# Strassen's seven products for gate and value of layer two

## The chip, the cores and the metric

The kernel runs on one core of one Trainium2 chip. The metric is the device time of one execution in microseconds (us), and lower is better. Each number stands for a median over executions. TensorE (PE) does the matmuls, VectorE (DVE) the elementwise work on two operands, ScalarE (ACT) activations and copies, GpSimd (POOL) one subtraction, and SyncE (SP) issues the DMAs.

## The reference, cut to what matters

An attention with a window and block sums feeds two layers, one after the other. The change touches the second layer, and the end of the first.

```python
def _moe_ref(x, w_in, w_out):                  # layer one: x 1536x512, d_ff 2048
    h = x @ w_in
    g = h * (1.0 / (1.0 + np.exp(-1.702 * h)))
    return (g @ w_out).astype(np.float32)

def _moe2_ref(x, w_gate, w_val, w_out):        # layer two: d_ff 1536
    gate = 1.0 / (1.0 + np.exp(-(x @ w_gate)))
    val = x @ w_val
    return (gate * val @ w_out).astype(np.float32)
```

The weights are double precision in memory.

## The kernel before

**Operands.** Every operand of a matmul is held as two tiles, a rounded high part and the low rest (`xH`, `xL`, `gh`, `gl`, and hi and lo of each weight). `mm3` (line 176) computes a product as three matmuls into one PSUM bank: low by high, high by low, high by high. Each matmul has a stationary operand of 128 x 128 and 512 moving columns.

**Tiling.** The 1536 tokens are three blocks of 512 (`blk`). The hidden width is cut into groups of 256 columns, two of 128 (`f`): eight groups in layer one, six in layer two. The 512 input features are four chunks of 128 (`kk`), so one `f` of one block is 4 x 3 = 12 matmuls.

**One step** is a layer, a group and a block. `first` (line 190) projects: in layer two, gate for `f` into one PSUM bank (line 218), its sigmoid on ACT (line 198), value for `f` into another bank (line 221), then their product on DVE (line 202), the rounded copy on ACT (line 203) and the rest on POOL (line 204). That is 48 matmuls in layer two and 24 in layer one. `second` (line 225) multiplies the hidden group by the output weights, four tiles `m` of 6 matmuls each, and adds every tile to an accumulator on DVE (line 260; for group 0 a copy on ACT, line 256). At the last group of layer one the accumulator becomes the input of layer two: `yH` is a copy on ACT (line 262), `yL` a subtraction on DVE (line 263).

**Weights.** `fetch` brings one matrix piece of 256 columns by two DMAs on SP's queue, one piece ahead. `decode` (line 92) makes hi and lo of it: six DVE instructions (lines 104, 108, 110, 112, 117, 119) and two ACT ones (105, 115), all 1024 wide. Layer two needs three pieces for a group.

**Order.** In the main loop (from line 561) each step issues `first` of this step and then `second` of the step before. A generator, `coming`, holds the decode; `pull` issues one piece of it between two parts of a step. The program's order gives priorities; a planner that models the engines then fixes each engine's order, and may put a ready instruction ahead of one that it takes to be late. SP's order stays as written. On the chip each engine runs its own order strictly. Tiles and PSUM banks come from rings: two banks named `h` for projections and six named `o` for the second product, and an instruction that reuses one waits for its last reader.

Of the kernel before, what the change touches and what calls it, by code (L numbers as in the profile page):

```python
# [8 lines left out]
F32 = mybir.dt.float32  # L9
F32R = mybir.dt.float32r  # L10
# [19 lines left out]
def attention_moe_moe2_kernel(ctx: ExitStack, tc: tile.TileContext, ins: dict, out: bass.AP):  # L30
# [34 lines left out]
    class Slots:  # L65


        def __init__(self, tag):
            self.tag, self.order, self.i = tag, [], 0
# [16 lines left out]
    pool([w_slots], 8, "w_a")  # L86
    pool([gh_slots, gl_slots], 1, "g_a")
# [4 lines left out]
    def decode(raw, mid, hi_out, lo_out):  # L92
# [26 lines left out]
        nc.vector.scalar_tensor_tensor(out=lo_out, in0=b, scalar=2.0 ** -36, in1=af, op0=ALU.mult, op1=ALU.mult)  # L119
        yield  # L120

    n1 = w_in.shape[1] // (GF * P)
# [16 lines left out]
    for layer, g in groups:  # L139
        for i, w in enumerate(mats[layer]):  # L140
            last = i == len(mats[layer]) - 1
            src = [rows_of(x, g) if last else cols_of(x, g, n) for x, n in ((w.bitcast(U32), 2), (w.bitcast(U16), 4))]
            pieces.append((f"{layer}_{g}_{i}", *src))

    def fetch():

        if pieces:
# [7 lines left out]
            nc.sync.dma_start(out=to[:, :, 0:2 * m - 1], in_=shifted[:, :, 1:])  # L155
            raws.append((raw, mid, (P, n, m // 2)))

    def load_group(layer, g):
        tiles = weights[layer, g] = []
        ready[layer, g] = 0  # L160
        for i in range(len(mats[layer])):
            raw, mid, shape = raws.pop(0)
            hi, lo = (w_slots.tile(list(shape), F32R, f"w{layer}_{g}_{i}{x}") for x in "HL")
            tiles += [hi, lo]
            parts = decode(raw, mid, hi.rearrange("p a n -> p (a n)"), lo.rearrange("p a n -> p (a n)"))
            for step, _ in enumerate(parts):
                if step == 1:

                    fetch()
                yield  # L170
            ready[layer, g] += 1
            yield

    acc, gt = {}, {}

# [8 lines left out]
    def project(wh, wl, f, blk, name):  # L184
        ps = ps_h.tile([P, TB], F32, tag="h", name=name)
        c = slice(f * P, (f + 1) * P)
        mm3(ps, [((wh[:, kk, c], wl[:, kk, c]), (xH[blk][:, kk, :], xL[blk][:, kk, :])) for kk in range(KC)])
        return ps

    def first(layer, g, blk, batch=False):  # L190
        w = weights[layer, g]
        gh = gh_slots.tile([P, GF, TB], F32R, f"gh{layer}_{g}_{blk}")
        gl = gl_slots.tile([P, GF, TB], F32R, f"gl{layer}_{g}_{blk}")
        gt[layer, g, blk] = gh, gl

        def sigmoid(layer, ps):
            sg = sg_slots.tile([P, TB], F32, "sg")
            nc.scalar.activation(sg, ps, AF.Sigmoid, scale=1.702 if layer == 1 else 1.0)  # L198
            return sg

        def gated(f, ps, sg):
            nc.vector.tensor_tensor(out=sg, in0=ps, in1=sg, op=ALU.mult)  # L202
            nc.scalar.copy(gh[:, f, :], sg)  # L203
            nc.gpsimd.tensor_tensor(out=gl[:, f, :], in0=sg, in1=gh[:, f, :], op=ALU.subtract)  # L204
# [12 lines left out]
        for f in range(GF):  # L217
            ps = project(w[0], w[1], f, blk, "ps_h")
            sg = sigmoid(layer, ps)
            if layer == 2:  # L220
                ps = project(w[2], w[3], f, blk, "ps_v")
            gated(f, ps, sg)
            yield

    def second(layer, g, blk, last, lag=False):
        w = weights[layer, g]
        wh, wl = w[-2], w[-1]
        gh, gl = gt.pop((layer, g, blk))
        if g == 0:
            acc[layer, blk] = (acc_a if blk < 2 else acc_b).tile([P, 4, 512], F32, tag=f"acc{blk}", name=f"acc{layer}_{blk}")  # L230
        a = acc[layer, blk]
        if layer == 1 and last:
            xH[blk] = xp.tile([P, KC, TB], F32R, tag="xH", name=f"yH{blk}")
            xL[blk] = xp.tile([P, KC, TB], F32R, tag="xL", name=f"yL{blk}")
        for m in range(4):
            ps = ps_o.tile([P, 512], F32, tag=o_tag, name="ps_o")
            c = slice(m * P, (m + 1) * P)
            if layer == 1:
                mm3(ps, [((wh[:, f, c], wl[:, f, c]), (gh[:, f, :], gl[:, f, :])) for f in range(GF)])
            elif last and blk == NTB - 1 and m == 3:  # L240

                r0 = blk * TB + m * P
                for n0 in range(0, 512, 256):
                    n = slice(n0, n0 + 256)
                    if n0:
                        ps = ps_o.tile([P, 512], F32, tag=o_tag, name="ps_o")
                    mm3(ps[:, n], [((gh[:, f, c], gl[:, f, c]), (wh[:, f, n], wl[:, f, n])) for f in range(GF)])
                    nc.vector.tensor_tensor(out=a[:, m, n], in0=ps[:, n], in1=a[:, m, n], op=ALU.add)
                    nc.sync.dma_start(out=out[r0:r0 + P, n], in_=a[:, m, n])
                return  # L250
            else:
                mm3(ps, [((gh[:, f, c], gl[:, f, c]), (wh[:, f, :], wl[:, f, :])) for f in range(GF)])
# [21 lines left out]
    def pull(n):  # L274
        for _ in range(n):
            if next(coming, True):
                break
# [281 lines left out]
            pull(2)  # L559

    with tc.manual_schedule(engines={mybir.EngineType.SP}):
        pool([w_slots], 4, "w_b")
        pool([gh_slots, gl_slots], 1, "g_b")
        pool([sg_slots], 2, "sg_b")
        acc_b = ctx.enter_context(tc.tile_pool(name="acc_b", bufs=1, reuse_waits="tile"))
        ps_o = ctx.enter_context(tc.tile_pool(name="ps_o", bufs=6, space=PSUM, reuse_waits="tile"))
        o_tag = "o"
        pull(1000)
        coming = load_group(*groups[2])
        pull(1)  # L570
        prev = None
        for step in steps[EARLY:]:
            layer, g, blk = step
            need(layer, g, len(mats[layer]) - 1)
            for _ in first(*step):
                pull(1)
            if prev:
                need(*prev[:2], len(mats[prev[0]]))
                for _ in second(*prev, prev[1] == ends[prev[0]]):
                    pull(1 if groups.index((layer, g)) + 1 < n1 else 2)  # L580
            prev = step
            nxt = groups.index((layer, g)) + 1
            if nxt < len(groups) and groups[nxt] not in ready and blk == (NTB - 1 if layer == 1 and g < 2 else 0):
                pull(1000)
                coming = load_group(*groups[nxt])
        for _ in second(*prev, True):
            pass

# [39 lines left out]
```

## Time and profile before

| | us |
|---|---|
| median of 3 runs | 664.73 (664.64 to 665.26) |
| span of the profiled execution, first to last instruction | 661.9 |
| TensorE busy | 631.7 (95%) |
| VectorE busy | 415.2 (63%) |
| ScalarE busy | 243.1 (37%) |
| GpSimd busy | 187.2 (28%) |

The device time holds the span and some microseconds around it: 664.73 - 661.9 = 2.8 us. Busy time is the union of an engine's instructions. Matmuls overlap, so the duration of one (0.39 us) is longer than the step from one start to the next; the step is the pace.

### The profile page before, as it was taken

The page shows a single profiled execution, that of the slowest core. Times are in us where ns is not written, and L with a number is a line of the kernel's source. Part 1 is how long each engine was busy: PE and PEld are TensorE (multiplying, and loading weights), DVE is VectorE, ACT ScalarE, POOL GpSimd, SP SyncE. Part 2 cuts the span into 40 slices and gives each one's busy share as a digit, 9 for nine tenths or more (in the row PEclk, how much of TensorE's full clock was granted, in tenths as well). Part 3 has the DMA queues.
Part 4 walks back from the last instruction along what each step waited for, and adds up shares of the span by engine and source line. Part 5 has one row for each costly group of instructions (what it writes and reads, how often), then busy time and mean ns, then how long its engine had stood idle before and what let it go on. Part 6 is the DMA issues. An engine that isn't in the chain of part 4 may idle for free.

```text
span 661.9 us, 8251 instructions
## 1 busy us (share of the span) xinstructions
PE 631.7 (95%) x3168; PEld 515.1 (78%) x3170; DVE 415.2 (63%) x604; ACT 243.1 (37%) x498; POOL 187.2 (28%) x164
## 2 busy tenths in 40 slices
PE   6478799999999999999999999999999999999997
PEld 3255688778888888888888888888888888888886
DVE  6899656559998777777778626437627627422223
ACT  3355574746443333333345425313213213211110
POOL 6574576413332222213131112111111111211110
PEclk9778899999999999999999999999999999999999
DMA  9999773007775242434333034423414413000013
GB/s 314 351 372 325 223 236 94 3 13 276 255 261 198 93 171 99 159 111 145 118 138 111 20 124 143 147 92 140 176 66 151 182 49 128 0 1 0 13 67 112
DMA packets 39672, 93.97 MB, mean 142 GB/s; under 512 B 2128, under 2 KB 12624, under 8 KB 39632
## 3 DMA queue, kind: packets, MB, share of 16 engines
q1 hardware_dynamic: 39056, 92.39, 40.3%
q10 hardware_dynamic: 576, 1.05, 0.4%
q8 instruction: 25, 0.41, 0.2%
q14 instruction: 15, 0.12, 0.1%
HBM read 88.71 MB, written 3.15 MB: 139 GB/s over the span
## 4 chain that ended last, share of the span: by engine, by line
PE 88%; DVE 3%; DMA 3%; ACT 3%; POOL 1%; issue 1%; SPq 0%; DVEq 0%; ACTq 0%; POOLq 0%
PE ps_o L181 35%; PE ps_h L181 34%; PE ps_v L181 15%; DMA mid<-in_moe_w_in 2%; PE ps_s L381 2%; PE ps_x L429 1%; PE ps_p L414 1%; ACT e L394 1%; DMA vt<-in_vt 1%; DVE nm L386 1%; POOL kx L370 0%; ACT L198 0%; ACT L394 0%; DVE dc L110 0%; DVE dc L112 0%
## 5 line engine op out<-in xcount | busy, mean ns | idle before, releaser
L204 POOL TENSOR_TENSOR gl<-sg,gh 128x512 fp32r<-128x512 f32 x84 | 116.1, 1383 | 419.4 <-ACT gh L203 419.3
L260 DVE TENSOR_TENSOR acc<-ps_o,acc 128x512 f32<-128x512 f32 x143 | 96.3, 684 | 37.2 <-PE ps_o L181 36.8
L203 ACT CAST gh<-sg 128x512 fp32r<-128x512 f32 x84 | 52.1, 621 | 134.9 <-DVE sg L202 134.9
L198 ACT ACTIVATE sg<-ps_h 128x512 f32<-128x512 f32 x84 | 49.8, 596 | 139.2 <-PE ps_h L181 139.1
L202 DVE TENSOR_TENSOR sg<-ps_v,sg 128x512 f32<-128x512 f32 x36 | 24.8, 690 | 110.5 <-PE ps_v L181 110.0
L181 PE MATMUL ps_o<-gl,w_1H 128*128 128x512 f32 x192 | 75.6, 394 | 0.7 <-POOL gl L204 0.7
L181 PE MATMUL ps_o<-gh,w_1L 128*128 128x512 f32 x192 | 75.6, 400 | 0.5 <-ACT gh L203 0.4
L181 PE MATMUL ps_h<-xL,w_0H 128*128 128x512 f32 x192 | 75.7, 394 | 0.0
L181 PE MATMUL ps_h<-xH,w_0L 128*128 128x512 f32 x192 | 75.3, 396 | 0.0
L181 PE MATMUL ps_h<-xH,w_0H 128*128 128x512 f32 x192 | 75.3, 392 | 0.0
L181 PE MATMUL ps_o<-gh,w_1H 128*128 128x512 f32 x192 | 75.1, 391 | 0.0
L181 PE MATMUL ps_o<-w_2L,gh 128*128 128x512 f32 (+1 forms) x146 | 56.4, 386 | 0.0
L181 PE MATMUL ps_o<-w_2H,gl 128*128 128x512 f32 (+1 forms) x146 | 56.4, 386 | 0.0
L181 PE MATMUL ps_o<-w_2H,gh 128*128 128x512 f32 (+1 forms) x146 | 56.4, 386 | 0.0
L181 PE MATMUL ps_h<-yH,w_0L 128*128 128x512 f32 x144 | 56.0, 389 | 0.0
L181 PE MATMUL ps_h<-yL,w_0H 128*128 128x512 f32 x144 | 56.0, 389 | 0.0
L181 PE MATMUL ps_h<-yH,w_0H 128*128 128x512 f32 x144 | 56.0, 389 | 0.0
L181 PE MATMUL ps_v<-yH,w_1L 128*128 128x512 f32 x144 | 56.0, 389 | 0.0
L181 PE MATMUL ps_v<-yL,w_1H 128*128 128x512 f32 x144 | 56.0, 389 | 0.0
L181 PE MATMUL ps_v<-yH,w_1H 128*128 128x512 f32 x144 | 56.0, 389 | 0.0
L202 DVE TENSOR_TENSOR sg<-ps_h,sg 128x512 f32<-128x512 f32 x48 | 32.8, 685 | 30.1 <-ACT sg L198 30.1
L112 DVE SCALAR_TENSOR_TENSOR dc<-da,dc 128x1024 uint32<-128x1024 uint32 x34 | 48.6, 1429 | 0.5
(80 smaller groups left out, 1077.0 us busy)
## 6 DMA issues: line engine op xcount, KB each, us to landing
raw<-in_moe_w_out SPq DMA_DIRECT2D x13, 1024.0 KB, 4.9
mid<-in_moe_w_out SPq DMA_DIRECT2D x13, 1023.5 KB, 6.8
raw<-in_moe_w_in SPq DMA_DIRECT2D x8, 1024.0 KB, 5.3
mid<-in_moe_w_in SPq DMA_DIRECT2D x8, 1023.0 KB, 7.2
raw<-in_moe_w_gate SPq DMA_DIRECT2D x6, 1024.0 KB, 5.1
raw<-in_moe_w_val SPq DMA_DIRECT2D x6, 1024.0 KB, 5.0
mid<-in_moe_w_gate SPq DMA_DIRECT2D x6, 1023.0 KB, 7.1
mid<-in_moe_w_val SPq DMA_DIRECT2D x6, 1023.0 KB, 7.1
```

What stands on the lines that cost most here:

```text
L112: nc.vector.scalar_tensor_tensor(out=c, in0=a, scalar=0x80000000, in1=c, op0=ALU.bitwise_and, op1=ALU.bitwise_or)
L181: nc.tensor.matmul(ps, lhsT=a, rhs=b, start=i == 0, stop=i == n - 1)
L198: nc.scalar.activation(sg, ps, AF.Sigmoid, scale=1.702 if layer == 1 else 1.0)
L202: nc.vector.tensor_tensor(out=sg, in0=ps, in1=sg, op=ALU.mult)
L203: nc.scalar.copy(gh[:, f, :], sg)
L204: nc.gpsimd.tensor_tensor(out=gl[:, f, :], in0=sg, in1=gh[:, f, :], op=ALU.subtract)
L260: nc.vector.tensor_tensor(out=a[:, m, :], in0=ps, in1=a[:, m, :], op=ALU.add)
L381: nc.tensor.matmul(ps[:, j, :], lhsT=t[:, j, :], rhs=kt[:, j, :], start=False, stop=j == G - 1)
L386: nc.vector.tensor_reduce(out=nm, in_=live["s", u], axis=AX.X, op=ALU.max, negate=True)
L394: nc.scalar.activation(e[:, j, :], s[:, j, :], AF.Exp, bias=nm[:, j:j + 1], accum_out=sm[:, j:j + 1])
L414: nc.tensor.transpose(ps[:, j, :], e[:, j, :], ident)
L429: nc.tensor.matmul(ps[64 * e:64 * e + 64, j, :], lhsT=vw(b, g * G + j)[:, h * D:(h + 1) * D], rhs=t[:, j, 64 * e:64 * e + 64], start=True, ...
```

## The change

For token blocks 0 and 1 of layer two, gate and value of a group are each a 2 x 2 problem: two `f` by two halves of the features (`LO`, `HI`) for the weights, two halves of the features by two token blocks for the input. The eight half products (6 matmuls each) are replaced by Strassen's seven. Block 2 is computed as before (`single`).

- **Weight sums.** `combine` makes four sums or differences of weight blocks for gate and for value of each group on DVE, from the sum of hi and lo, and splits them again into hi (ACT) and lo (DVE).
- **Token sums.** `token_sums` makes four differences of halves of blocks 0 and 1 of layer two's input once, at the end of layer one, on DVE, and splits them. Two of the four tiles m of block 1 are not turned into `yH`, `yL` for it.
- **Recombination.** Products that share an output add up in one PSUM bank. Product 1 is also copied from bank to bank by ACT. Products 5 and 6 are kept in SBUF by ACT, and DVE adds two totals from PSUM and SBUF for gate and for value.
- **Order.** The last two groups of layer one run blocks 0 and 1 of both before block 2 of either. In layer two a group is `pair` (14 products, with `second` of block 2 of the group before between them) and then `single` (with `second` of blocks 0 and 1). Projections now take the six `o` banks, and `second` the two `h` banks. The weights are decoded in another order, with `w_out` of a group behind the gate piece of the next.
- **Memory.** The gated tiles are one `f` each, five of them; there are seven `sg` tiles instead of four and two more weight tiles. Weight sums have one set of four tiles.

```diff
-    steps += [(layer, g, blk) for layer, g in groups[2:] for blk in range(NTB)]
+    steps += [(1, g, blk) for g in range(2, n1 - 2) for blk in range(NTB)]
+    steps += [(1, g, blk) for g in (n1 - 2, n1 - 1) for blk in range(2)] + [(1, g, 2) for g in (n1 - 2, n1 - 1)]
...
+    wanted = [(1, g, i) for g in range(n1) for i in range(2)] + [(2, 0, 0), (2, 0, 1)]
+    for g in range(n2):
+        wanted += [(2, g + 1, 0)] * (g + 1 < n2) + [(2, g, 2)] + [(2, g + 1, 1)] * (g + 1 < n2)
...
+    def combine(g, i):
+        hi, lo = weights[2, g, i]
+        w, s = (wtmp.tile([P, KC, GF * P], F32, tag=t, name=f"{n}{g}_{i}") for t, n in (("da", "wf"), ("db", "ws")))
+        nc.vector.tensor_tensor(out=w.rearrange(flat), in0=hi.rearrange(flat), in1=lo.rearrange(flat), op=ALU.add)
+        yield
...
+            nc.vector.tensor_tensor(out=s[:, n], in0=a, in1=b, op=op)
...
+        nc.scalar.copy(sh.rearrange(flat), s.rearrange(flat))
+        nc.vector.tensor_tensor(out=sl.rearrange(flat), in0=s.rearrange(flat), in1=sh.rearrange(flat), op=ALU.subtract)
...
+    def prepare():
+        for g in range(-1, n2):
+            for n in ([0, 1] if g < 0 else [0, 2, 1]):
+                to = g + (n != 2)
+                if to < n2:
+                    weights[2, to, n] = yield from load(Ring(w_c if n == 2 else w_a), 2, to, n)
+                    ready[2, to, n] = 1
+                    yield
+            for n in range(2 * (g + 1 < n2)):
+                yield from combine(g + 1, n)
...
+    def token_sums():
...
+            nc.vector.tensor_tensor(out=to, in0=x, in1=y, op=ALU.subtract)
...
+            nc.scalar.copy(h, to)
+            yield
+            nc.vector.tensor_tensor(out=l, in0=to, in1=h, op=ALU.subtract)
...
+    def pair(g):
...
+        for n in "1256734":
+            for i in range(2):
+                b = bank[n]
+                p = new(b, i) if n in "15" else ps[b, i]
+                product(p, left[n](i), right[n], n in "15")
+                if n == "1":
+                    nc.scalar.copy(new("y", i), p)
+                elif n == "2":
+                    out(i, (0, 0), p)
+                elif n == "5":
+                    keep("5", i, p)
+                elif n == "6":
+                    keep("6", i, p)
+                elif n == "7":
+                    t = total("5", i, p)
+                    out(i, (1, 1), t, t)
+                elif n == "3":
+                    t = total("6", i, p)
+                    out(i, (1, 0), t, t)
+                else:
+                    out(i, (0, 1), p)
+                yield
...
-            if last and layer == 1:
+            if last and layer == 1 and blk == 1 and m < KC // 2:
+                pass
+            elif last and layer == 1:
...
+                if prev == (1, n1 - 1, 1):
+                    folding = token_sums()
...
+            elif step == (1, n1 - 1, 0):
+                pull(1000)
+                coming = prepare()
+        ps_f, ps_o, o_tag = ps_o, ps_h, "h"
...
+        for g in range(n2):
+            for key in ((2, g, 0), (2, g, 1), (2, g, "s", 0), (2, g, "s", 1)):
+                while key not in ready:
+                    pull(1)
+            for _ in folding:
+                pass
+            rest = second(*prev, prev[0] == 1)
+            for slot, _ in enumerate(pair(g)):
+                ahead(g + 1)
+                if slot % 2:
+                    next(rest, None)
+                if slot % 4 == 3:
+                    ahead(g + 1)
...
+            rest = (x for blk in range(2) for x in second(2, g, blk, g == ends[2]))
+            for _ in single(g):
+                ahead(g + 1)
+                next(rest, None)
+                ahead(g + 1)
...
+            prev = (2, g, 2)
```

## Rows read from the trace of the kernel before

**Rows 1.** Span and mean granted TensorE clock of the core.
```profile
core 0: 661.9 us, clock 0.982
```

**Rows 2.** The page: busy time by engine, then the chain that ended last, by engine.
```profile
PE 631.7 (95%) x3168; PEld 515.1 (78%) x3170; DVE 415.2 (63%) x604; ACT 243.1 (37%) x498; POOL 187.2 (28%) x164
...
PE 88%; DVE 3%; DMA 3%; ACT 3%; POOL 1%; issue 1%; SPq 0%; DVEq 0%; ACTq 0%; POOLq 0%
```

**Rows 3.** Stages: length, busy us and instructions of each engine, clock, DMA share, GB/s.
```profile
326.00:359.00 33.00, 33.00 (x147) 27.35 (x146) 26.83 (x36) 14.24 (x21) 8.09 (x6) 1.00 0.35 129
...
449.00:498.00 49.00, 49.00 (x218) 40.58 (x217) 27.69 (x36) 13.46 (x18) 7.89 (x6) 1.00 0.36 129
...
359.00:645.00 286.00, 286.00 (x1263) 236.89 (x1262) 137.63 (x179) 78.58 (x114) 47.05 (x35) 1.00 0.26 92
```

**Rows 4.** TensorE in order of time in layer two: start us, duration us.
```profile
643.72 0.39 PE L181 MATMUL ps_h<-yH,w_0L 128*128 128x512 f32 x1
...
646.44 0.39 PE L181 MATMUL ps_o<-w_2L,gh 128*128 128x512 f32 x1
646.67 0.39 PE L181 MATMUL ps_v<-yH,w_1L 128*128 128x512 f32 x1
...
649.16 0.39 PE L181 MATMUL ps_v<-yH,w_1H 128*128 128x512 f32 x1
```

**Rows 5.** Groups of instructions by line, 385 to 645 us: busy us, mean ns.
```profile
L204 POOL TENSOR_TENSOR gl<-sg,gh 128x512 fp32r<-128x512 f32 x32 | 43.0, 1343 | 217.8 <-ACT gh L203 217.8
L260 DVE TENSOR_TENSOR acc<-ps_o,acc 128x512 f32<-128x512 f32 x53 | 36.4, 688 | 21.3 <-PE ps_o L181 20.9
...
L202 DVE TENSOR_TENSOR sg<-ps_v,sg 128x512 f32<-128x512 f32 x32 | 22.1, 690 | 100.7 <-PE ps_v L181 100.2 <-ACT da L105 0.5
L203 ACT CAST gh<-sg 128x512 fp32r<-128x512 f32 x32 | 19.9, 622 | 79.5 <-DVE sg L202 79.5
...
L112 DVE SCALAR_TENSOR_TENSOR dc<-da,dc 128x1024 uint32<-128x1024 uint32 x11 | 15.7, 1426 | 0.2
...
L117 DVE TENSOR_SCALAR da<-dc 128x1024 uint32<-128x1024 uint32 x11 | 10.0, 908 | 0.1
L104 DVE TENSOR_SCALAR da<-raw 128x1024 f32<-128x1024 f32 x11 | 7.6, 691 | 0.3
...
L119 DVE SCALAR_TENSOR_TENSOR w_0L<-db,da 128x1024 fp32r<-128x1024 uint32 x4 | 4.9, 1224 | 13.0 <-PE ps_h L181 13.0
L115 ACT CAST w_0H<-dc 128x1024 fp32r<-128x1024 f32 x4 | 4.2, 1056 | 10.6 <-PE ps_h L181 10.6
```

**Rows 6.** One line each: yL (ns min, median, max), then by-line row of xL.
```profile
L263 DVE TENSOR_TENSOR yL<-acc,yH x12: 675/680/1339, 346.8 to 377.8; 128x512 fp32r<-128x512 f32 x12
...
L450 DVE TENSOR_TENSOR xL<-ps_x,xH 128x256 fp32r<-128x256 f32 x24 | 9.9, 411 | 4.9 <-ACT xH L447 4.8
```

**Rows 7.** VectorE and GpSimd in order of time, group 1 of layer two.
```profile
401.84 1.23 DVE L119 SCALAR_TENSOR_TENSOR w_0L<-db,da 128x1024 fp32r<-128x1024 uint32 x1 [4.22 <-PE ps_h L181]
...
424.06 2.21 DVE L119 SCALAR_TENSOR_TENSOR w_2L<-db,da 128x1024 fp32r<-128x1024 uint32 x1 [1.25 <-PE ps_o L181]
...
423.88 1.31 POOL L204 TENSOR_TENSOR gl<-sg,gh 128x512 fp32r<-128x512 f32 x1 [6.87 <-ACT gh L203]
```

**Rows 8.** The last gating: VectorE, ScalarE and GpSimd in order of time.
```profile
649.69 0.69 DVE L202 TENSOR_TENSOR sg<-ps_v,sg 128x512 f32<-128x512 f32 x1 [5.98 <-PE ps_v L181]
...
650.41 0.62 ACT L203 CAST gh<-sg 128x512 fp32r<-128x512 f32 x1 [3.17 <-DVE sg L202]
...
651.11 1.30 POOL L204 TENSOR_TENSOR gl<-sg,gh 128x512 fp32r<-128x512 f32 x1 [6.62 <-ACT gh L203]
```

**Rows 9.** DMA issues from 300 us on: KB each, median us from issue to landing.
```profile
mid<-in_moe_w_gate SPq DMA_DIRECT2D x5, 1023.0 KB, 7.2
```

More of the change, by code (lines that the diff above doesn't have):

```diff
@@ L120, in decode, with product @@
         yield
+    LO, HI = slice(0, KC // 2), slice(KC // 2, KC)
+    def product(ps, a, b, start):
+        n = 3 * (KC // 2)
+        i = 0
+        for kk in range(KC // 2):
+            for x, y in ((1, 0), (0, 1), (0, 0)):
+                nc.tensor.matmul(
+                    ps, lhsT=a[x][:, kk, :], rhs=b[y][:, kk, :],
+                    start=start and i == 0, stop=i == n - 1, skip_group_check=True,
+                )
+                i += 1
     n1 = w_in.shape[1] // (GF * P)
@@ L138, in attention_moe_moe2_kernel @@
     pieces, weights, raws, ready = [], {}, [], {}
[L139 to L143, printed above, removed]
+    wanted = [(1, g, i) for g in range(n1) for i in range(2)] + [(2, 0, 0), (2, 0, 1)]
+    for g in range(n2):
+        wanted += [(2, g + 1, 0)] * (g + 1 < n2) + [(2, g, 2)] + [(2, g + 1, 1)] * (g + 1 < n2)
+    for layer, g, i in wanted:
+        w = mats[layer][i]
+        last = i == len(mats[layer]) - 1
+        src = [rows_of(x, g) if last else cols_of(x, g, n) for x, n in ((w.bitcast(U32), 2), (w.bitcast(U16), 4))]
+        pieces.append((f"{layer}_{g}_{i}", *src))
     def fetch():
@@ L156, in fetch, with load @@
             raws.append((raw, mid, (P, n, m // 2)))
+    def load(slots, layer, g, i):
+        raw, mid, shape = raws.pop(0)
+        hi, lo = (slots.tile(list(shape), F32R, name=f"w{layer}_{g}_{i}{x}") for x in "HL")
+        parts = decode(raw, mid, hi.rearrange("p a n -> p (a n)"), lo.rearrange("p a n -> p (a n)"))
+        for step, _ in enumerate(parts):
+            if step == 1:
+                fetch()
+            yield
+        return hi, lo
     def load_group(layer, g):
@@ L161, in load_group @@
         for i in range(len(mats[layer])):
[L162 to L170, printed above, removed]
+            tiles += yield from load(w_slots, layer, g, i)
@@ new lines, in attention_moe_moe2_kernel @@
+    sums = {}
+    def prepare():
[5 more added lines that the diff above has]
+                    ready[2, to, n] = 1
+                    yield
+            for n in range(2 * (g + 1 < n2)):
+                yield from combine(g + 1, n)
+                ready[2, g + 1, "s", n] = 1
+    def token_sums():
+        a, b = acc[1, 0], acc[1, 1]
+        for name, x, y, to in (
+            ("1", b[:, LO], a[:, LO], a[:, LO]),
+            ("3", b[:, HI], b[:, LO], b[:, LO]),
+            ("2", b[:, HI], a[:, LO], b[:, HI]),
+            ("4", a[:, HI], b[:, HI], a[:, HI]),
+        ):
+            nc.vector.tensor_tensor(out=to, in0=x, in1=y, op=ALU.subtract)
+            if name == "4":
+                h, l = xH[1][:, LO], xL[1][:, LO]
+            else:
+                h, l = (tp.tile([P, KC // 2, TB], F32R, tag=f"t{name}{x}", name=f"t{name}{x}") for x in "HL")
+            nc.scalar.copy(h, to)
+            yield
+            nc.vector.tensor_tensor(out=l, in0=to, in1=h, op=ALU.subtract)
+            tsum[name] = h, l
+            yield
@@ new lines, in attention_moe_moe2_kernel, with sums_of, a, new @@
+    tsum = {}
+    def pair(g):
+        def sums_of(n, i):
+            return tuple(x[:, n] for x in sums[g, i])
+        def a(i, r, c):
+            return tuple(block(x, r, c) for x in weights[2, g, i])
+        b11, b21, b22 = ((xH[n][:, h], xL[n][:, h]) for n, h in ((0, LO), (0, HI), (1, HI)))
+        left = {
+            "1": lambda i: a(i, 0, 0), "2": lambda i: a(i, 0, 1), "3": lambda i: sums_of(3, i),
+            "4": lambda i: a(i, 1, 1), "5": lambda i: sums_of(0, i), "6": lambda i: sums_of(1, i),
+            "7": lambda i: sums_of(2, i),
+        }
+        right = {"1": b11, "2": b21, "3": b22, "4": tsum["4"], "5": tsum["1"], "6": tsum["2"], "7": tsum["3"]}
+        bank = {"1": "x", "2": "x", "5": "v", "3": "v", "6": "y", "7": "y", "4": "y"}
+        ps, held, sg = {}, {}, {}
+        def new(b, i):
+            ps[b, i] = ps_f.tile([P, TB], F32, tag="o", name=f"ps_{b}")
+            return ps[b, i]
+        def keep(n, i, p):
+            held[n, i] = sg_slots.tile([P, TB], F32, "sg")
+            nc.scalar.copy(held[n, i], p)
+        def total(n, i, p):
+            nc.vector.tensor_tensor(out=held[n, i], in0=p, in1=held[n, i], op=ALU.add)
+            return held[n, i]
+        def out(i, to, x, own=None):
+            if i:
+                gate_by((2, g, *to), x, sg.pop(to))
+                return
+            sg[to] = own if own is not None else sg_slots.tile([P, TB], F32, "sg")
+            nc.scalar.activation(sg[to], x, AF.Sigmoid)
+        for n in "1256734":
[17 more added lines that the diff above has]
+                    out(i, (1, 0), t, t)
+                else:
+                    out(i, (0, 1), p)
+                yield
@@ new lines, in single @@
+    def single(g):
+        for f in range(GF):
+            sg = None
+            for i in range(2):
+                wh, wl = weights[2, g, i]
+                ps = ps_f.tile([P, TB], F32, tag="o", name="ps_h" if i == 0 else "ps_v")
+                for j in range(2):
+                    half = (LO, HI)[j]
+                    product(ps, (block(wh, f, j), block(wl, f, j)), (xH[2][:, half], xL[2][:, half]), j == 0)
+                    if j == 0:
+                        yield
+                if i == 0:
+                    sg = sg_slots.tile([P, TB], F32, "sg")
+                    nc.scalar.activation(sg, ps, AF.Sigmoid)
+                else:
+                    gate_by((2, g, 2, f), ps, sg)
+                yield
@@ L188, in project, with gate_by @@
         return ps
+    def gate_by(to, val, sg):
+        name = "_".join(map(str, to))
+        gh = gh_slots.tile([P, TB], F32R, f"gh{name}")
+        gl = gl_slots.tile([P, TB], F32R, f"gl{name}")
+        gt[to] = gh, gl
+        nc.vector.tensor_tensor(out=sg, in0=val, in1=sg, op=ALU.mult)
+        nc.scalar.copy(gh, sg)
+        nc.gpsimd.tensor_tensor(out=gl, in0=sg, in1=gh, op=ALU.subtract)
     def first(layer, g, blk, batch=False):
         w = weights[layer, g]
-        gh = gh_slots.tile([P, GF, TB], F32R, f"gh{layer}_{g}_{blk}")
-        gl = gl_slots.tile([P, GF, TB], F32R, f"gl{layer}_{g}_{blk}")
-        gt[layer, g, blk] = gh, gl
         def sigmoid(layer, ps):
@@ L201, in gated @@
         def gated(f, ps, sg):
-            nc.vector.tensor_tensor(out=sg, in0=ps, in1=sg, op=ALU.mult)
-            nc.scalar.copy(gh[:, f, :], sg)
-            nc.gpsimd.tensor_tensor(out=gl[:, f, :], in0=sg, in1=gh[:, f, :], op=ALU.subtract)
+            gate_by((layer, g, blk, f), ps, sg)
         if batch:
@@ L218, in first @@
             ps = project(w[0], w[1], f, blk, "ps_h")
[L219 to L222, printed above, removed]
+            gated(f, ps, sigmoid(layer, ps))
             yield
     def second(layer, g, blk, last, lag=False):
-        w = weights[layer, g]
-        wh, wl = w[-2], w[-1]
-        gh, gl = gt.pop((layer, g, blk))
+        wh, wl = weights[layer, g][-2:] if layer == 1 else weights[2, g, 2]
+        gh, gl = zip(*(gt.pop((layer, g, blk, f)) for f in range(GF)))
         if g == 0:
@@ L238, in second @@
             if layer == 1:
-                mm3(ps, [((wh[:, f, c], wl[:, f, c]), (gh[:, f, :], gl[:, f, :])) for f in range(GF)])
+                mm3(ps, [((wh[:, f, c], wl[:, f, c]), (gh[f], gl[f])) for f in range(GF)])
             elif last and blk == NTB - 1 and m == 3:
@@ L246, in second @@
                         ps = ps_o.tile([P, 512], F32, tag=o_tag, name="ps_o")
[L247 removed]
+                    mm3(ps[:, n], [((gh[f][:, c], gl[f][:, c]), (wh[:, f, n], wl[:, f, n])) for f in range(GF)])
                     nc.vector.tensor_tensor(out=a[:, m, n], in0=ps[:, n], in1=a[:, m, n], op=ALU.add)
@@ L251, in second @@
             else:
-                mm3(ps, [((gh[:, f, c], gl[:, f, c]), (wh[:, f, :], wl[:, f, :])) for f in range(GF)])
+                mm3(ps, [((gh[f][:, c], gl[f][:, c]), (wh[:, f, :], wl[:, f, :])) for f in range(GF)])
             if lag:
@@ L576, in attention_moe_moe2_kernel, with ahead @@
                 pull(1)
+                next(folding, None)
             if prev:
                 need(*prev[:2], len(mats[prev[0]]))
-                for _ in second(*prev, prev[1] == ends[prev[0]]):
-                    pull(1 if groups.index((layer, g)) + 1 < n1 else 2)
+                for _ in second(*prev, prev[1] == ends[1]):
+                    pull(1)
+                    next(folding, None)
+                if prev == (1, n1 - 1, 1):
+                    folding = token_sums()
             prev = step
-            nxt = groups.index((layer, g)) + 1
-            if nxt < len(groups) and groups[nxt] not in ready and blk == (NTB - 1 if layer == 1 and g < 2 else 0):
+            if blk == (NTB - 1 if g < 2 else 0) and (1, g + 1) in groups and (1, g + 1) not in ready:
                 pull(1000)
-                coming = load_group(*groups[nxt])
+                coming = load_group(1, g + 1)
+            elif step == (1, n1 - 1, 0):
+                pull(1000)
+                coming = prepare()
+        ps_f, ps_o, o_tag = ps_o, ps_h, "h"
+        def ahead(g):
+            if (2, g, "s", 1) not in ready:
+                pull(1)
+        for g in range(n2):
+            for key in ((2, g, 0), (2, g, 1), (2, g, "s", 0), (2, g, "s", 1)):
+                while key not in ready:
+                    pull(1)
+            for _ in folding:
[7 more added lines that the diff above has]
+                    ahead(g + 1)
+            for _ in rest:
+                pass
+            while (2, g, 2) not in ready:
+                pull(1)
+            rest = (x for blk in range(2) for x in second(2, g, blk, g == ends[2]))
[3 more added lines that the diff above has]
+                ahead(g + 1)
+            for _ in rest:
+                pass
+            prev = (2, g, 2)
         for _ in second(*prev, True):
```

34 lines of the change are left out of this document (27 added, 7 removed).

## The prediction

> **What bounds the kernel now.** I read the cores first: one core, 661.9 us, granted clock 0.982 [rows 1], so nothing disturbed has to be set aside. Then the busy shares and the chain of waits [rows 2]: TensorE is busy 95% and carries 88% of the chain; VectorE, at 63%, is 3% of it. An average over the program says little, so I went to the stages. From 359 to 645 us, layer two, TensorE is busy for the whole 286 us at clock 1.00, its 2.4 GHz level, while VectorE is busy 137.6 us, ScalarE 78.6 and GpSimd 47.0 [rows 3]. Being busy need not mean running at pace, so I looked at starts: from 643.72 to 646.44 us there are 12 matmuls, 2.72 us, 0.2267 us for each [rows 4]. One group of layer two is 3 x (48 + 24) = 216 matmuls, 49.0 us at that pace, and the stretch of 49 us from 449 holds 218 (those cut by its edges count twice). So matmuls follow each other without a gap, and a matmul less is 0.2267 us less, as long as nothing else comes late. The same rows show a matmul of the second product put between gate and value at 646.44: the planner fills TensorE with other ready work, which will matter below.
>
> **What is removed.** For gate and for value, a group's two blocks cost 8 half products of 6 matmuls; now 7. That is 6 matmuls less, twice for a group, in six groups: 72 matmuls x 0.2267 = 16.3 us. Shape and moving width stay, so the pace does too. A group becomes 204 matmuls, 46.2 us: 108 in the paired part (24.5 us) and 96 in the rest (21.8 us). This is the whole of the gain.
>
> **What VectorE gets.** The trace has no plain sum of two SBUF operands that is 1024 wide. The 256-wide subtraction takes 411 ns, the 512-wide 680 (median), 269 ns for 256 columns more [rows 6]; so 1024 columns come to 0.68 + 2 x 0.269 = 1.22 us, and the 1024-wide L119 with two SBUF operands takes 1.224 [rows 5]. Two 512-wide ones at their worst would be 2.7 us; I take 1.22. Weight sums of one matrix are 1.22 + 4 x 0.41 + 1.22 = 4.1 us, twice for a group 8.2 us. The totals are four instructions like L202 (0.69), 2.8 us. The token sums are four times two 1024-wide ones, 9.8 us, once. Two yL of block 1 go away, 1.4 us less.
>
> *A whole group.* VectorE was busy 27.7 us of 49 [rows 3]; now 27.7 + 8.2 + 2.8 = 38.7 of 46.2 us, 84%. By itself that fits beside TensorE. ScalarE gets two bank copies and four keeps (six of about 0.62) and two 1024-wide copies (1.056) [rows 5]: 13.5 + 5.8 = 19.3 us of 46.2. GpSimd keeps its six subtractions of 1.34 [rows 5]. The weight DMAs are the same eighteen pieces of layer two, 7.2 us to landing [rows 9], and a group has 46 us for three. All of these I cost at nothing; their cover is TensorE's stream, and it is gone where VectorE fills up. That is once:
>
> *The boundary of the layers.* Take the stretch from the start of the projections of group 6, block 1, to the end of group 0 of layer two. TensorE has five steps of layer one (5 x 48) + 108 + 96 = 444 matmuls, 100.7 us. VectorE has to do in it: seven decodes (w_in and w_out of group 7, gate and value of groups 0 and 1, w_out of group 0), each 3 x 0.69 + 1.43 + 0.91 + 1.22 = 5.6 us (L108 and L110 taken as L104) [rows 5], 39.4 us; four matrices of weight sums, 16.4; token sums, 9.8; 24 accumulations at 0.69, 16.6; 10 yL at 0.68, 6.8; 20 gatings and totals at 0.69, 13.8. That is 102.8 us against 100.7: no room. In the last steps of layer one VectorE was at 26.8 of 33 us, 81% [rows 3], and these now also hold the sums. What lets it slip is that the weight sums of group 1 are wanted only at product 5, after products 1 and 2 and two tiles m, 36 matmuls or 8.2 us into the group. So the excess of 2.1 us is free if VectorE never waits; if its efficiency is 0.9, it needs 114 us, and 114 - 100.7 - 8.2 = 5 us of stall. Inside the stretch the nearest risk is product 5 of group 0: the first two steps give VectorE about as much as it can do (5.6 + 2.8 + 1.4 us and more of 10.9 for one), and the last holds three token sums and the first weight sums. It waits for token sum 1 and weight sums 0, in program order done a microsecond or so before; value's sums come some 4 us later, and the planner can put products 6, 7 and 3 of gate ahead. Bounds for the boundary: 0 and 10 us (the upper from the collisions weighed next). I take 3.
>
> *Collisions.* When GpSimd's gl is running, L119 takes 2.21 us instead of 1.23 [rows 7], and yL goes from 680 to 1339 [rows 6]; instructions that read PSUM, such as L260 and L202, stay at 0.69. The price is up to 1 us for each gl. The Trainium skill (SBUF — State Buffer, section Who interferes with whom) says that a VectorE instruction with two SBUF inputs contends with a GpSimd instruction that reads SBUF; the trace agrees, 2.21 against 1.23 us, and by that rule every weight and token sum of this change is exposed. In a full group six collisions would make 38.7 + 6 = 44.7 us of 46.2, still no bound. At the boundary there are 16 gl; at 0.6 us more than my durations hold for each, VectorE needs 112.4 us, which leaves 3.5 us of stall; at the full 1 us each, 118.8, and 118.8 - 108.9 = 9.9 us.
>
> *PSUM and other waits.* Each second product now has two banks. In the unpaired part one tile m comes every 12 matmuls (2.72 us), so a bank is wanted again 5.44 - 1.36 = 4.1 us after its last matmul; the accumulation takes 0.69 and some 0.15 to begin, which leaves VectorE 3.2 us of slack. Products 7 and 4 share bank y: between 7 and 4 of the same matrix lie three half products, 4.1 us, for a total of 0.69 us. Product 4 ends the paired part, and its low part is wanted 9 matmuls later (2.0 us), while gating, copy and subtraction take from 649.16 + 0.39 to 652.41, 2.9 us [rows 4, 8]; the projections behind it are ready and can be put ahead, as at 646.44. I take 0.1 us for each of five groups, 0.5 us; bounds 0 and 1 us each.
>
> *The end.* The last gating is again followed by 2.9 us of chain, now with one tile m and two halves (12 matmuls, 2.7 us) to cover it, where before four tiles of block 1 stood there. I take 0.5 us, bounds 0 and 1.5.
>
> **The sum.** On the profiled execution: 661.9 - 16.3 + 3.0 + 0.5 + 0.5 = 649.6 us of span. The median of the runs lies 664.7 - 661.9 = 2.8 us above that span, which nothing here changes: **652.4 us**, 1.9% less. The likeliest case's own range is 648.4 (no stall at all) to 656.
>
> **The rivals.**
>
> *VectorE becomes the bound at the boundary and is slow to recover.* Collisions at the full price (9.9 us) and group 1 beginning behind: 664.7 - 16.3 + 9.9 + 1 = 659.3 us. For it: 102.8 against 100.7 us, and the rows of 2.21 us. Against: L119 for the gate pieces shows none (mean 1.224), a late VectorE still has other ready work, and a full group gives back 7.5 us. Chance 0.17, from 656 to 663.
>
> *Slower: VectorE's queue waits in order, in front of banks that are now two.* Its decode stood 4.22 us before L119 at 401.84, waiting for TensorE to free a weight tile [rows 7]; all accumulations behind it in the queue waited too. Before, six banks covered that. With two, each wait beyond 3.2 us stops TensorE, and weight sums have one set of tiles, whose last reader is product 3, so there are five such stores in a group (gate, value, w_out, two sums). If each waits 4.2 us there is 1 us of stall for each, 5 us for a group; over five groups 25 us: 664.7 - 16.3 + 25 + 1 = 674. It decides from 3.6 us for a group. Against it: the planner puts ready work in front of what it takes to be late, the sums come after product 3 by the program's order, and only some of the decodes showed such a wait. Chance 0.11, 666 and more.
>
> *The saving is eaten.* Smaller stalls of both kinds, about 2.5 us a group, or the matmuls running at a slower pace with sums as operands: 664.7 +- 1.3. The operands keep type and stride, which speaks against the second. Chance 0.05.
>
> That the seventy-two matmuls don't go away would need the planner to add work, which it doesn't do; no chance given.
>
> **How the numbers follow.** Likeliest 0.67 (648.4 to 656), VectorE bound 0.17 (656 to 663), the saving eaten 0.05, slower 0.11. A measurement of this kernel tells 0.2% (1.3 us) from no change. Faster is the first two, 0.84; within 0.2% 0.05; slower 0.11. The range from 648 to 662 leaves out the slower cases, the eaten saving and a little of the second: about 2 in 10.
>
> **What would show it.** Right: 72 fewer matmuls, starts still 0.2267 us apart in layer two, groups 1 to 4 46.2 us from product 1 to product 1, VectorE near 84% there, and the only gaps of TensorE in the paired part of group 0 and before the last four tiles, released by VectorE (sums or totals). Wrong: gaps in every group, in front of `ps_o` released by the accumulation, or in front of product 5 by the sums; more than 10 us of gaps at the boundary; a granted clock below 1.00 after such a gap; or layer one moved by its new order, whose end I take to stay where it was.

## The result and the profile after

The kernel after takes 648.74 us (median of 4 runs, 648.26 to 650.39) against 664.98 beside it: ratio 0.9765, 95% interval 0.9748 to 0.9781. That is 16.2 us less; 652.4 had been forecast, in a range of 648 to 662.

The page of the kernel after: busy time by engine, then the chain by engine.

```profile
PE 619.0 (96%) x3096; PEld 504.7 (78%) x3098; DVE 487.4 (75%) x706; ACT 277.1 (43%) x548; POOL 199.5 (31%) x164
...
PE 85%; DVE 8%; ACT 3%; DMA 2%; issue 1%; POOL 0%; SPq 0%; ACTq 0%; DVEq 0%; POOLq 0%
```

Against [rows 2], TensorE has 3168 - 3096 = 72 instructions less, VectorE 102 more and 72.2 us more of work; ScalarE has 34.0 us more.

The stages of the kernel after, with the columns of [rows 3]: the boundary of the layers, then a row for each of groups 1 to 4 of layer two, cut about where product 1 of each begins (the row of group 2 starts 3 us ahead of it), and the four together.

```profile
344.00:404.00 60.00, 60.00 (x266) 49.67 (x266) 58.36 (x73) 32.96 (x48) 14.98 (x9) 1.00 0.36 123
...
397.24:443.00 45.76, 45.76 (x203) 37.89 (x203) 28.63 (x36) 22.41 (x36) 9.65 (x6) 1.00 0.39 138
443.00:489.60 46.60, 46.60 (x207) 38.45 (x206) 38.67 (x50) 18.08 (x26) 10.05 (x6) 1.00 0.40 136
489.60:536.80 47.20, 46.80 (x206) 38.40 (x206) 39.57 (x55) 19.11 (x27) 9.06 (x6) 1.00 0.40 134
536.80:583.00 46.20, 46.20 (x205) 38.26 (x204) 40.24 (x53) 18.65 (x26) 10.20 (x6) 1.00 0.39 137
397.24:583.00 185.76, 185.36 (x817) 152.99 (x817) 147.12 (x191) 78.24 (x114) 38.96 (x24) 1.00 0.39 136
```

On average a group takes 46.4 us (185.76 / 4), forecast 46.2; from product 1 to product 1 it is 43.6 to 49.0 us, since the planner moves matmuls from one group into the time of another. VectorE is busy 36.8 us of a group on average (147.12 / 4), 79%: 63% in the row of group 1, 83 to 87% in the others. At the boundary it is busy 97%, with TensorE busy throughout. TensorE in order of time shows layer two's first projection, then the only wait in layer two that the trace names, then the end:

```profile
359.00 0.39 PE L131 MATMUL ps_x<-yH,w_0L 128*128 128x512 f32 x1
...
490.78 0.39 PE L131 MATMUL ps_x<-yH,w_0H 128*128 128x512 f32 x1
491.57 0.50 PE L359 MATMUL ps_o<-w_2H,gl 128*128 128x512 f32 x1 [0.40 <-DVE acc L439]
...
641.91 0.28 PE L359 MATMUL ps_o<-w_2H,gh 128*128 128x256 f32 x1
642.27 0.38 PE L359 MATMUL ps_o<-w_2H,gl 128*128 128x256 f32 x1
...
642.96 0.28 PE L359 MATMUL ps_o<-w_2H,gh 128*128 128x256 f32 x1
```

VectorE's accumulations in front of these two late starts:

```profile
490.83 0.68 DVE L439 TENSOR_TENSOR acc<-ps_o,acc 128x512 f32<-128x512 f32 x1
...
641.52 0.69 DVE L439 TENSOR_TENSOR acc<-ps_o,acc 128x512 f32<-128x512 f32 x1 [0.67 <-PE ps_o L359]
```

From 490.78 to 491.57 a start comes 0.79 us after the last, 0.56 more than the pace: the second product waits for a bank that VectorE's accumulation still holds, until 491.51. At the end 0.24 us are lost (0.36 from start to start where such a half takes 0.12). The profile names no releaser there, but the matmul at 642.27 begins the next use of one of the two banks right after the accumulation that ends at 642.21 (641.52 + 0.69). The account: in the kernel before, 299.2 us lie between layer two's first projection and its last matmul (358.58 to 657.75); now 284.0 (359.00 to 642.96), with 72 matmuls less between them. With the two losses of 0.8 us that is 16.0 of the 16.3 us that 72 matmuls are worth. Layer two begins 0.4 us later in this execution, so the spans differ by 15.4.

### The profile page after: what moved, and what is told of

Read it like the earlier page. It is cut to its first block, busy times and chain, and to the rows that moved or that the text cites. A ratio compares the mean times of both kernels' runs of the same rounds, so it can differ in the third digit from the quotient of the medians.

```text
span 646.5 us, 8331 instructions
## 1 busy us (share of the span) xinstructions
PE 619.0 (96%) x3096; PEld 504.7 (78%) x3098; DVE 487.4 (75%) x706; ACT 277.1 (43%) x548; POOL 199.5 (31%) x164
## 4 chain that ended last, share of the span: by engine, by line
PE 85%; DVE 8%; ACT 3%; DMA 2%; issue 1%; POOL 0%; SPq 0%; ACTq 0%; DVEq 0%; POOLq 0%
PE ps_o L359 35%; PE ps_h L359 20%; PE ps_v L131 9%; PE ps_y L131 7%; PE ps_x L131 5%; PE ps_h L131 4%; PE ps_s L562 2%; DMA q<-in_q 1%; PE ps_x L610 1%; DVE dc L112 1%; PE ps_p L595 1%; ACT e L575 1%; DMA vt<-in_vt 1%; DVE dc L110 1%; DVE sg L374 1%
## 5 line engine op out<-in xcount | busy, mean ns | idle before, releaser
L376 POOL TENSOR_TENSOR gl<-sg,gh 128x512 fp32r<-128x512 f32 x84 | 127.7, 1523 | 389.6 <-ACT gh L375 360.5
L383 ACT ACTIVATE sg<-ps_h 128x512 f32<-128x512 f32 x48 | 28.3, 595 | 55.7 <-PE ps_h L359 55.7
L105 ACT ACTIVATE da<-da 128x1024 f32<-128x1024 f32 x34 | 36.1, 1061 | 27.9 <-DVE da L104 27.9
L359 PEld LDWEIGHTS ps_o<-gh,w_1L 128*128 128x128 f32 x192 | 36.2, 189 | 11.4 <-ACT gh L375 3.7
L112 DVE SCALAR_TENSOR_TENSOR dc<-da,dc 128x1024 uint32<-128x1024 uint32 x34 | 44.4, 1307 | 0.6
L575 ACT ACTIVATE e<-ps_s,nm 128x128 f32<-128x128 f32 x96 | 34.0, 369 | 23.6 <-PE ps_p L595 11.8
L359 PEld LDWEIGHTS ps_o<-gl,w_1H 128*128 128x128 f32 x192 | 36.4, 190 | 8.3 <-POOL gl L376 1.0
L359 PEld LDWEIGHTS ps_h<-xH,w_0L 128*128 128x128 f32 x192 | 36.1, 189 | 8.1 <-ACT xH L628 0.6
L359 PEld LDWEIGHTS ps_h<-xL,w_0H 128*128 128x128 f32 x192 | 36.2, 189 | 7.6
L359 PEld LDWEIGHTS ps_h<-xH,w_0H 128*128 128x128 f32 x192 | 36.3, 189 | 7.5
```

The lines of the kernel that those rows point to most:

```text
L105: nc.scalar.activation(af, af, AF.Copy, scale=REBIAS)
L112: nc.vector.scalar_tensor_tensor(out=c, in0=a, scalar=0x80000000, in1=c, op0=ALU.bitwise_and, op1=ALU.bitwise_or)
L359: nc.tensor.matmul(ps, lhsT=a, rhs=b, start=i == 0, stop=i == n - 1)
L376: nc.gpsimd.tensor_tensor(out=gl, in0=sg, in1=gh, op=ALU.subtract)
L575: nc.scalar.activation(e[:, j, :], s[:, j, :], AF.Exp, bias=nm[:, j:j + 1], accum_out=sm[:, j:j + 1])
```

## The experiments

**The order alone, and the sums taken away.** The first kernel puts plain products in `pair`'s place:

```diff
+    def classic(g):
+        for f, n in ((0, 0), (1, 1), (1, 0), (0, 1)):
+            for i in range(2):
...
+                for j in range(2):
+                    half = (LO, HI)[j]
+                    product(ps, (block(wh, f, j), block(wl, f, j)), (xH[n][:, half], xL[n][:, half]), j == 0)
...
-            for slot, _ in enumerate(pair(g)):
+            for slot, _ in enumerate(classic(g)):
```

> The new order, rings and banks, but the paired part computes its eight half products for gate and for value plainly (96 matmuls in place of 84), without weight sums, token sums, keeps and totals. Theory (the gain is the 72 matmuls alone, TensorE never waits in either kernel): 664.7 us, within 1.3 of the kernel before. Rival (part of the gain comes from the new order, the one-f tiles or the six banks for projections): below 663; if it were half of the gain, 656.5.

664.31 us against 664.89, ratio 0.9991 (0.9978 to 1.0004). TensorE has 3170 instructions, and no wait is named from 300 us on. The new order, rings and banks are worth nothing by themselves. This kernel also keeps the smaller DMA scratch area (`dynamic_dma_scratch_size=1024`) that the kernel after asks for and that the list of the change leaves out, so that is worth nothing either.

The second kernel keeps the 84 matmuls and drops the sums:

```diff
-            return tuple(x[:, n] for x in sums[g, i])
+            return a(i, n // 2, n % 2)
...
-                yield from combine(g + 1, n)
...
-                    folding = token_sums()
```

> Strassen's 84 matmuls stay, but they read unsummed blocks: no weight sums and no token sums on VectorE and ScalarE; keeps, bank copies and totals stay (the output is not the layer's). Theory (the sums lie wholly beside TensorE): 648.7 us, within 1.0. Rival (VectorE's sums still cost something at the boundary of the layers): lower than 647.5; had the 3.0 us of the prediction been paid, 645.7.

648.22 us, ratio 0.9743 (0.9726 to 0.976), not to be told from the change itself. Its stages, boundary and group 2:

```profile
344.00:404.00 60.00, 60.00 (x267) 49.67 (x266) 43.23 (x57) 29.93 (x46) 12.53 (x10) 1.00 0.40 140
443.00:489.60 46.60, 46.60 (x207) 38.61 (x206) 30.30 (x38) 15.56 (x24) 9.07 (x6) 1.00 0.35 124
```

VectorE has 15.1 us less to do in the 60 us of the boundary (less the sums, more the two yL of block 1, which this kernel makes) and 8.4 less in the group; TensorE's column is the same. The sums are hidden to within what can be measured.

**Half of the groups.** `pair(g) if g < 3 else classic(g)`, with no weight sums for the rest; block 1 of groups 3 to 5 then reads token sums where its own input stood.

> Groups 0 to 2 of layer two by seven products, groups 3 to 5 by eight plain ones in the same order; 36 matmuls less instead of 72. Theory (each group of seven products gives its own 2.7 us, and nothing is lost at the boundary): 664.9 - 8.2 = 656.7, within 1. Rival (the boundary costs, so the first half gives less than the second): 658 or more.

656.42 us, ratio 0.9872 (0.9851 to 0.9894): 8.4 us less for 36 matmuls (8.2). The gain goes with the number of matmuls, and the first groups, with the boundary in them, give their share.

**How much room VectorE has.** In one kernel each VectorE instruction of `combine` of groups 1 to 5 is issued twice:

```diff
             nc.vector.tensor_tensor(out=s[:, n], in0=a, in1=b, op=op)
+            if g > 0:
+                nc.vector.tensor_tensor(out=s[:, n], in0=a, in1=b, op=op)
```

> Each VectorE instruction of the weight sums of groups 1 to 5 is issued twice: 8.2 us more of VectorE for each of these groups, so about 45 of the 46.2 us of a group by the trace (36.5 + 8.2). Theory (VectorE has 20% of slack and only its sum matters): 0 to 2 us a group of stall, 649 to 657, most likely 652. Rival (two banks for the second product and in-order waits make TensorE stop well before VectorE is full): 3 us a group or more, over 662.

659.11 us, ratio 0.9903 (0.9887 to 0.992): 10.4 us over the kernel after, 2.1 for each group, just outside the theory's bound. Group 2 and a stretch with most of the waits:

```profile
443.00:489.60 46.60, 46.60 (x206) 38.32 (x205) 45.19 (x62) 18.82 (x26) 11.79 (x7) 1.00 0.39 136
480.00:560.00 80.00, 75.04 (x320) 60.34 (x319) 77.03 (x103) 26.83 (x39) 18.19 (x11) 0.98 0.30 105
```

In group 2 VectorE is busy 97%, 6.5 us more than in the kernel after, and TensorE still never waits. The first wait comes at about 500 us, in group 3; in the 80 us from 480 on TensorE stands for 5 us. Its waits by releaser, from 300 us on (total, times, longest):

```profile
PE ps_o L365 <- DVE acc L445: 5.3, 4, 2.6
PE ps_v L131 <- DVE sL L236: 1.0, 2, 0.6
```

The waits are 6.3 of the 10.4 us; of the rest, a part is slower starts (0.43 us apart behind the longest wait). So the place is mainly the one that the slower rival named, the two banks of the second product, but it costs more than the 0.8 us of the kernel after only where VectorE is full. The other kernel moves `gl` of layer two from GpSimd to VectorE:

```diff
-        nc.gpsimd.tensor_tensor(out=gl, in0=sg, in1=gh, op=ALU.subtract)
+        (nc.vector if to[0] == 2 else nc.gpsimd).tensor_tensor(out=gl, in0=sg, in1=gh, op=ALU.subtract)
```

> The low part gl of layer two's gated tiles is computed on VectorE instead of GpSimd: 4.1 us a group more of VectorE (six times 0.69), no collisions in layer two. Theory (VectorE has about 6.7 us of slack a group, and TensorE's pace is all that counts): 648.7 within 1. Rival (GpSimd's collisions cost something now): below 647.5. Rival (two banks, in-order waits): 2 us or more above 648.7.

648.15 us, ratio 0.975 (0.9725 to 0.9774), and no wait is named from 300 us on. But this is no test of the slack, for VectorE hardly got busier. Four groups, from product 1 of group 1 on:

```profile
396.50:581.40 184.90, 184.90 (x817) 153.13 (x816) 148.59 (x215) 78.22 (x113) 0.00 (x0) 1.00 0.38 136
```

That is 148.59 us where the kernel after has 147.12: 0.4 us a group, not 4.1. The added instructions are there, 24.6 us for all six groups, but the sums no longer run beside GpSimd: the mean of L215 falls from 1.38 to 1.22 us over the run. So `gl` on VectorE is nearly free for VectorE itself. Of the slack the first kernel alone tells: about 8 us more a group cost 2 us a group; how much less would be free was not measured.

**What the planner's order is worth.** TensorE's order is kept as written from the main loop on: `engines={SP, PE}` for `engines={SP}` in the second `manual_schedule`.

> From the second half of the program on, TensorE's order is kept as written; the planner still orders the other engines. Theory (the planner's putting ready matmuls ahead is what hides VectorE's lateness): product 4's low part is wanted 2.0 us after its last matmul and is there after 2.9, so at least 0.9 us a group, and the boundary shows its 0 to 10 us: 655 to 664. Rival (there is slack enough in the written order): 648.7 within 1.5.

679.1 us, ratio 1.0207 (1.0187 to 1.0226): slower than the kernel before, and 30.4 us over the kernel after, twice the most that I had allowed. TensorE around the wait of group 1:

```profile
436.68 0.39 PE L359 MATMUL ps_o<-w_2H,gh 128*128 128x512 f32 x1
441.24 0.79 PE L359 MATMUL ps_o<-w_2H,gl 128*128 128x512 f32 x1 [4.17 <-POOL gl L376]
441.83 0.63 PE L359 MATMUL ps_o<-w_2L,gh 128*128 128x512 f32 x1
442.26 0.63 PE L359 MATMUL ps_o<-w_2H,gh 128*128 128x512 f32 x1
442.69 0.63 PE L131 MATMUL ps_h<-yH,w_0L 128*128 128x512 f32 x1
```

GpSimd and VectorE meanwhile, and the stage behind the wait with its clock:

```profile
436.87 4.32 POOL L376 TENSOR_TENSOR gl<-sg,gh 128x512 fp32r<-128x512 f32 x2 [1.89 <-ACT gh L375]
...
436.65 1.21 DVE L119 SCALAR_TENSOR_TENSOR w_1L<-db,da 128x1024 fp32r<-128x1024 uint32 x1
437.90 2.17 DVE L215 TENSOR_TENSOR wf<-w_0H,w_0L 128x1024 f32<-128x1024 f32 x1
...
440.00:460.00 20.00, 18.76 (x71) 15.26 (x72) 18.04 (x27) 5.94 (x8) 2.74 (x2) 0.83 0.32 106
```

This is the low part of product 4. I had counted 0.9 us of wait. Two gl stand in a row, since VectorE's gatings of products 3 and 4 come one right behind the other, and beside VectorE's decode and weight sum they take 4.32 us together, where one takes 1.29 alone. The gap is 4.33 us over the pace, the longest of the seven. In the last group, where VectorE has no next group to prepare, it is 0.98, about what I had counted. And behind the wait shown the starts are 0.43 us apart instead of 0.2267: TensorE is at its 1.2 GHz level, and the mean granted clock of the 20 us is 0.83. Over the trace from 300 us on, seven gaps make 21.5 us and slower starts 9.5, together the 30 us.

The same done to the kernel before:

> The kernel before with TensorE's order kept as written from the main loop on, as was done to the kernel after (679.1 us there). Theory (in the kernel before, every low part is wanted a whole second product, 5.4 us, after it starts, so the planner's order is worth little there): 664.9 to 668. Rival (a written order costs any of these kernels tens of us): 680 or more.

664.39 us, ratio 0.9995 (0.998 to 1.001), no wait named from 300 us on. The kernel before needs no help; the change does. A written order with block 1 ahead of block 0 behind each paired part (`for blk in (1, 0)`):

> TensorE's order as written, as in the run that took 679.1 us, but the second product of block 1 is written ahead of that of block 0 behind each paired part, so that the low part of product 4 (block 0) is wanted 24 matmuls of second product and 24 of projection later, and the first one wanted is that of product 3. Theory (the loss of 30 us was the wait for product 4's low part, and the slower clock behind it): most of it goes, 650 to 660. Rival (many small waits spread over the group): over 668.

669.81 us, ratio 1.0066 (1.0042 to 1.0089): 9 us came back, far fewer than expected. The time is the rival's, but its many small waits are not there: the trace names seven, 13.5 us in all. Here is group 1's:

```profile
436.32 0.39 PE L131 MATMUL ps_h<-yH,w_0H 128*128 128x512 f32 x1
439.36 0.50 PE L359 MATMUL ps_o<-w_2H,gl 128*128 128x512 f32 x1 [2.65 <-POOL gl L376]
```

Product 3's low part is nearly as late as product 4's (gaps of 2.2 to 2.8 us a group instead of 3.0 to 4.3): it first has to pass a total, a sigmoid and a gating behind VectorE's queue, and its gl takes 2.07 us beside VectorE's work. So one swap doesn't replace the planner.

**The boundary.** In the prediction VectorE had no room there, and yet nothing was lost. The trace of the kernel after shows where the weight sums of group 0 stand:

```profile
291.44 1.21 DVE L215 TENSOR_TENSOR wf<-w_0H,w_0L 128x1024 f32<-128x1024 f32 x1
296.31 1.23 DVE L215 TENSOR_TENSOR wf<-w_1H,w_1L 128x1024 f32<-128x1024 f32 x1
305.43 1.22 DVE L230 TENSOR_TENSOR sL<-ws,sH 128x1024 fp32r<-128x1024 f32 x1
```

They begin 68 us before layer two. In the next kernel they can't:

```diff
+        if g == 0:
+            nc.vector.tensor_copy(w[:, 0, 0:P], acc[1, 0][:, 3, 0:P])
         nc.vector.tensor_tensor(out=w.rearrange(flat), in0=hi.rearrange(flat), in1=lo.rearrange(flat), op=ALU.add)
```

> A copy of 128 columns from the finished accumulator of block 0 of layer one goes ahead of the weight sums of group 0 into their work tile, so VectorE can't make them before about 348 us (they stand at 291 to 306 us in the kernel after). That is the place where the prediction had put them. Theory (the boundary was free because the planner made the decodes and sums a group ahead): the 8.2 us come on top of a stretch in which VectorE is busy 58.4 of 60 us, and TensorE waits 1 to 8 us: 650 to 657, most likely 652. Rival (the boundary has room anyway, because TensorE takes other work): 648.7 within 1.

650.38 us, ratio 0.9777 (0.9754 to 0.98). The interval overlaps that of the change, so the time alone decides nothing; the trace does in part. The sums now stand at 340.54 to 361.3, and TensorE waits once in the stretch, for 1.02 us, behind ScalarE's copy of an accumulator:

```profile
344.00:404.00 60.00, 58.98 (x260) 48.53 (x259) 59.06 (x78) 32.91 (x48) 17.78 (x10) 1.00 0.30 106
...
400.74 0.50 PE L361 MATMUL ps_o<-w_2H,gl 128*128 128x512 f32 x1 [1.02 <-ACT acc L437]
...
304.70:405.50 100.80, 99.78 (x441) 82.30 (x440) 79.48 (x109) 45.43 (x68) 27.60 (x16) 1.00 0.18 63
```

With VectorE at 59.06 of 60 us, the boundary costs 1 us, not 3. Both answers may hold something: the early sums spare that 1 us, and TensorE's other ready work covers the rest. But the test is weaker than it was meant to be. In the whole stretch of the prediction (last row) VectorE is busy 79.5 us, no more than in the kernel after (82.4): other work moved out as the sums moved in. A boundary with the 102.8 us of the prediction was not run, and what it would cost stays open.

**Is there more to win?** `gl` on VectorE and block 1 first, under the planner, beside the kernel after once more:

> The planner orders TensorE again; gl of layer two on VectorE and block 1 ahead of block 0. Theory (TensorE waits about 1 us in all of layer two, so there is nothing more to win): 648.3 within 0.8, not to be told from the kernel after. Rival (small waits and collisions still cost): below 647.3.

> The kernel after, unchanged, on the chip of the kernel with gl on VectorE and swapped blocks: 648.7 within 0.7 by every theory.

648.17 us (0.9755, 0.9741 to 0.9769) and 649.39 us (0.9772, 0.9758 to 0.9785). The intervals overlap; no version is shown to be faster than the change.

## Why the prediction was right, and where it was off

- *72 matmuls at 0.2267 us, 16.3 us:* right. 72 instructions fewer, 16.0 us by the account of layer two, nothing from the order alone, half of it for half of the groups.
- *VectorE at 38.7 us a group, 84%:* near; 36.8 us (79%) on average over groups 1 to 4, of which 28.6 in the row of group 1 and 38.7, 39.6 and 40.2 us in the others. The collisions are there, and on both sides, where the prediction had charged them to VectorE alone: weight sums L215 have a mean of 1.41 us in layer two where 1.22 was taken, and gl rose from a mean of 1.38 to 1.52 us over the whole run. They fit into the slack, as they were said to.
- *The boundary, 3.0 us:* the term that was mis-sized; no wait was measured there. The step that failed is the inventory, "VectorE has to do in it: seven decodes ... four matrices of weight sums". I had taken the place of each instruction from the program's order. In the kernel after, VectorE is busy 82.4 us in that stretch, where I had counted 102.8 (its stage, with the columns of [rows 3]):

```profile
304.70:405.50 100.80, 100.80 (x447) 83.45 (x446) 82.38 (x109) 48.40 (x72) 24.85 (x16) 1.00 0.26 87
```

The trace of the kernel before could have told: there the low part of the gate weights of group 0 is written 70 us before layer two begins:

```profile
288.06 1.82 DVE L119 SCALAR_TENSOR_TENSOR w_0L<-db,da 128x1024 fp32r<-128x1024 uint32 x1 [1.34 <-PE ps_h L181]
```

- *0.5 us for the groups and 0.5 for the end:* 0.56 and 0.24 measured, but the agreement is luck. Both terms stood for a low part that comes late (product 4's, the last gating's), and no such wait is named in layer two. What was lost is two waits for one of the two banks of the second product, which is the slower rival's mechanism.
- *2.8 us around the span:* 648.74 - 646.5 = 2.2 here. The difference is not a fixed cost: a median was set against the span of one execution. In each of the four runs of the kernel after its own time lies 1.8 us above its own span. The 3.0 us that weren't lost and these 0.6 us make up nearly all of the 3.7 us between forecast and result.
- *The slower rival:* the banks cost the 0.8 us above, and more where VectorE had less room: 1.4 us with the late sums, 5.3 us with the doubled ones. What would have turned the change into a loss is the wait that I had dismissed in half a sentence, product 4's low part, priced at 0.9 us a group in written order and worth 3.0 to 4.3 us and a slower clock. That "the projections behind it are ready and can be put ahead" is the sentence on which the whole gain stood; it held.

## What to carry to other kernels

Where TensorE issues without gaps, a matmul taken away gives its pace back, and the extra elementwise work can be free as long as the engine that does it keeps some slack. Try how much is left by doubling the work, and read from the trace by how much the engine really got busier: here 8 us more a group cost 2 us a group, while the six instructions a group moved over from GpSimd cost VectorE 0.4 us and not the 4.1 of their own time. Where a planner sets the order, read from the trace how far ahead of the program it runs an engine before adding up a stretch. And look for the tightest distance from a result to its reader: it decides whether the change depends on that order.

## What the runs showed of the hardware

TensorE's clock after a wait, in layer two: behind the four waits of 3.9 to 4.2 us in the kernel with TensorE's order as written, starts were 0.43 us apart, its 1.2 GHz level. Behind all waits up to 1.3 us they went back to 0.23 to 0.24 us. In between, the length of the wait didn't tell. In that same kernel the wait of group 0, 2.79 us, was followed by full pace; with the blocks swapped, the wait of group 0, 2.04 us, was followed by the 1.2 GHz level, and so was that of 2.65 us, after a few starts at 0.23 to 0.39 us. First the kernel as written, then the swapped one:

```profile
390.54 0.50 PE L359 MATMUL ps_o<-w_2H,gl 128*128 128x512 f32 x1 [2.79 <-POOL gl L376]
...
391.10 0.40 PE L359 MATMUL ps_o<-w_2H,gh 128*128 128x512 f32 x1
391.34 0.39 PE L131 MATMUL ps_h<-yH,w_0L 128*128 128x512 f32 x1
...
388.57 0.50 PE L359 MATMUL ps_o<-w_2H,gl 128*128 128x512 f32 x1 [2.04 <-POOL gl L376]
...
389.25 0.63 PE L359 MATMUL ps_o<-w_2H,gh 128*128 128x512 f32 x1
389.68 0.63 PE L359 MATMUL ps_o<-w_2H,gl 128*128 128x512 f32 x1
```

VectorE and GpSimd: at the wait of 4.17 us each collision lengthened the instruction that began second. VectorE's L119 was under way when the first gl began, and kept its 1.21 us; that gl took 2.12 us instead of 1.29 alone. The addition of two 1024-wide SBUF operands (L215) began while it ran and took 2.17 us instead of 1.21. The second gl began beside that addition and took 2.24.
